# Two-stream attention block on one core: the text gate and text output as one run of 32-column tiles, and the first scales by a transpose

## The chip, the cores and the metric

The kernel runs on one core of a Trainium2 chip. A core has a matrix engine (TensorE), a vector engine (VectorE), a scalar engine (ScalarE), GpSimd and SyncE, and 16 DMA engines which move data between HBM and the on-chip memory SBUF. Matmuls write to a second on-chip memory, PSUM, from which VectorE or ScalarE must take the result ("empty" it). The metric is the device time of one execution in microseconds, the median of several runs. In the profile PE is TensorE's matmuls, PEld its weight loads, DVE VectorE, ACT ScalarE, POOL GpSimd, SP SyncE.

## What is computed

Two streams of tokens, image and text, are normalised, scaled and shifted by vectors made from a conditioning vector `c`, projected to q, k and v, joined for one attention, and projected back with a gate. The reference, cut to what matters:

```python
# B, Ni, Nt, D = 2, 256, 32, 1152; all inputs bf16
mod_i = (silu(c) @ wmod_img).reshape(B, 6, 1, D)      # mod_t likewise from wmod_txt
shi, sci, gai = mod_i[:, 0], mod_i[:, 1], mod_i[:, 2]
sht, sct, gat = mod_t[:, 0], mod_t[:, 1], mod_t[:, 2]
hi = layernorm(x_img) * (1 + sci) + shi
ht = layernorm(x_txt) * (1 + sct) + sht
qkvi, qkvt = hi @ wqkv_img, ht @ wqkv_txt             # split into q, k, v; text and image joined
p = softmax(einsum('bqd,bkd->bqk', q, k) * D ** -0.5)
a = einsum('bqk,bkd->bqd', p, v)
out_i = x_img + gai * (a[:, Nt:] @ wo_img)
out_t = x_txt + gat * (a[:, :Nt] @ wo_txt)
```

## The kernel before

The contraction over D = 1152 runs in KT = 9 steps of 128 rows (`kt` or `dt`). The kernel begins with the layer norm of four image tiles (128 tokens each), transposes them, scales them by `1 + sci` and starts the product for v. Weights stream in on SyncE's DMA queue in the order of use, into five slots that are reused. `pin` keeps an instruction in program order on its engine.

The scales are a product of `silu(c)` with a weight block. `sc_rows` makes them as rows, with four 32-column tiles of the matrix engine side by side (`tile_position`), into `sc_ps`; a VectorE transpose (`sc_cols`) turns them into columns. For the first 128 features the kernel before also makes a column directly, with matmuls two columns wide, and scales the first block from PSUM:

```python
def sc_first(r0, r1):
    if r0 == 0:
        mm(sc0_ps[:], lhsT=warm[:, 0:P], rhs=unit[:, 0:B], start=True, stop=False)
    for kt in range(r0, r1):
        mm(sc0_ps[:], lhsT=w_sc_i[:, kt, 0:P], rhs=sT[:, kt, :], start=False, stop=(kt == KT - 1))

def x_scale(k0, k1, b, step=TPB, first=False):
    for kt in range(k0, k1):
        for t in range(0, TPB, step):
            t0, t1 = b * NI + t * P, b * NI + (t + step) * P
            pin(nc.vector.tensor_scalar(hS_i[:, kt, t0:t1], xT_i[:, kt, t0:t1],
                                        sc0_ps[:, b:b + 1] if first else sc1_i[:, kt, b:b + 1], None,
                                        op0=ALU.mult))
...
sc_rows(0, 4)
sc_first(0, 4)
warm_up(2)                                  # matmuls without use[...]
...                                         # transposes of image tiles 2 and 3 in three parts
sc_first(7, K8)                             # K8 = KT - 1: the last two weight rows
sc_first(K8, KT)
sc_rows(7, KT)
x_scale(0, 1, 0, step=1, first=True)
sc_cols(0, 5)
x_scale(1, 3, 0)
v_open(A0, 0, 3)                            # the first v matmuls, names vps<-t,hS_i
```

The end: the image output is made in four tiles of 128 tokens, each in chunks of up to 384 columns. A chunk is nine matmuls, then a multiplication by the gate out of PSUM (`tmp`) and an addition of x (`o`), both on VectorE. The text gate is one row per batch (`mod_rows`, nine sets of four 32-column matmuls, name `gps`); ScalarE copies it out, GpSimd's DMA queue writes it to DRAM and reads it back spread over the partitions (`gbf`). In the kernel before it runs behind the first chunk of output tile 1, and the text output, with 64-column tiles, between output tiles 2 and 3:

```python
def mod_rows(w_blk):
    gps = ps_mm.tile([P, VC], f32, tag="mm")                    # VC = 288
    for kt in range(KT):
        for g in range(NGG):                                    # NGG = 4
            mm(gps[32 * g:32 * g + 32, :], lhsT=sT32[:, kt, :], rhs=w_blk[:, kt, g * VC:(g + 1) * VC],
               start=(kt == 0), stop=(kt == KT - 1), tile_position=(0, 32 * g))
    return gps

def out_img(i, chunks, parts=None, between=None):
    ...
    for n in chunks:
        if c0 and between:
            between = between()
        ps = ps_mm.tile([P, CH], f32, tag="mm")                 # CH = 384
        for dt in range(KT):
            mm(ps[:, 0:n], lhsT=aT[:, dt, t0:t0 + P], rhs=w_o_i[:, dt, c0:c0 + n],
               start=(dt == 0), stop=(dt == KT - 1))
        tmp = work.tile([P, CH], bf, tag="tmp")
        nc.vector.tensor_mul(tmp[:, 0:n], ps[:, 0:n], gb[:, b, c0:c0 + n])
        nc.vector.tensor_add(o[:, c0:c0 + n], tmp[:, 0:n], x_i[:, i, c0:c0 + n])
        ...                                                     # store of the finished columns

def out_txt():
    of = work.tile([P, 2, VC], bf, tag="of", bufs=1)
    for r in range(2):
        ps = ps_mm.tile([P, VC], f32, tag="mm")
        for dt in range(KT):
            for g in range(2):
                c0 = (2 * r + g) * VC
                mm(ps[64 * g:64 * g + NTT, :], lhsT=aT[:, dt, NI:NI + NTT], rhs=w_o_t[:, dt, c0:c0 + VC],
                   start=(dt == 0), stop=(dt == KT - 1), tile_position=(0, 64 * g))
        tmp = work.tile([P, CH], bf, tag="tmp")
        nc.vector.tensor_mul(tmp[:, 0:VC], ps[:], gbf[:, r, :])
        nc.vector.tensor_add(of[:, r, :], tmp[:, 0:VC], xf[:, r, :])
    ...                                                         # two stores

w_ga_t = load_w(3, wmod_txt, 2 * D)                             # the text gate's weights
w_o_t = load_rows(1, wo_txt, 0, (0, 5))                         # the last weights: dt 0 to 4, then 5 to 8
...
out_img(0, C3)
out_img(1, C3, between=txt_gate)
out_img(2, C3)
out_txt()
out_img(3, (CH, CH, 224, 160), parts=(2 * CH, D - 160, D))
```

Of the kernel before, what the change touches and what calls it, by code (L numbers as in the profile page):

```python
# [14 lines left out]
def kernel(  # L15
# [26 lines left out]
    NTT = B * NT  # L42
    CH = 384
    NCH = D // CH
    VC = 288
# [7 lines left out]
    work = ctx.enter_context(tc.tile_pool(name="work", bufs=2))  # L53
    small = ctx.enter_context(tc.tile_pool(name="small", bufs=4))
    ps_mm = ctx.enter_context(tc.tile_pool(name="ps_mm", bufs=6, space=PSUM))
    ps_tr = ctx.enter_context(tc.tile_pool(name="ps_tr", bufs=2, space=PSUM))

    pin = tc.keep_in_program_order

    def mm(*a, **k):  # L60
        return pin(nc.tensor.matmul(*a, **k))  # L61

    def tr(*a, **k):
        return pin(nc.tensor.transpose(*a, **k))  # L64
# [6 lines left out]
    x_i = act.tile([P, NIT, D], bf)  # L71
# [10 lines left out]
    K8 = KT - 1  # L82
# [17 lines left out]
    w_sc_i = wtile(0)  # L100
# [21 lines left out]
    warm = const.tile([P, 512], bf)  # L122
# [3 lines left out]
    unit = const.tile([P, LW], bf)  # L126
# [41 lines left out]
    sT = const.tile([P, KT, B], bf)  # L168
# [46 lines left out]
    hS_i = act.tile([P, KT, B * NI], bf, tag="Bt")  # L215
    xT_i = act.tile([P, KT, B * NI], bf)
# [8 lines left out]
        pin(nc.vector.transpose(t[:].rearrange("p c l -> p (c l)"), gps[:].rearrange("p c l -> p (c l)")))  # L225
        return t

    sc0_ps = ps_mm.tile([P, B], f32, tag="mm")
    tp60 = ps_mm.tile([P, 3, NI], bf, tag="mm", name="tp")
    tp61 = ps_mm.tile([P, 3, NI], bf, tag="mm", name="tp")  # L230
    sc_ps = ps_mm.tile([P, KT, LW], f32, tag="mm")

    def sc_first(r0, r1):
        if r0 == 0:
            mm(sc0_ps[:], lhsT=warm[:, 0:P], rhs=unit[:, 0:B], start=True, stop=False)
        for kt in range(r0, r1):
            mm(sc0_ps[:], lhsT=w_sc_i[:, kt, 0:P], rhs=sT[:, kt, :], start=False, stop=(kt == KT - 1))

    def sc_rows(r0, r1):
        if r0 == 0:  # L240
            for g in range(NGG):
                mm(sc_ps[LW * g:LW * g + LW].rearrange("p c l -> p (c l)"), lhsT=unit[:], rhs=warm[:, 0:KT * LW],
                   start=True, stop=False, tile_position=(0, LW * g))
        for kt in range(r0, r1):
            for g in range(NGG):
                mm(sc_ps[LW * g:LW * g + LW], lhsT=sT32[:, kt, :], rhs=group(w_sc_i, kt, g),
                   start=False, stop=(kt == KT - 1), tile_position=(0, LW * g))

    def x_tiles(k0, b):
        return (tp61 if b else tp60) if k0 == 6 else ps_tr.tile([P, 3, NI], bf, tag="tr", name="tp")  # L250

    def x_transposes(tp, k0, b, ts=range(TPB)):
        for kt in range(k0, k0 + 3):
            for t in ts:
                i = b * TPB + t
                tr(tp[:, kt - k0, t * P:(t + 1) * P], xn_i[:, i, kt * P:(kt + 1) * P], ident[:])

    def x_out(tp, k0, b):
        dst = xT_i[:, k0:k0 + 3, b * NI:(b + 1) * NI]
        pin(nc.vector.tensor_copy(dst, tp[:]) if k0 == 3 else nc.scalar.copy(dst, tp[:]))  # L260

    sc1_i = const.tile([P, KT, LW], f32, name="scc", tag="scc")

    def sc_cols(c0, c1):
        pin(nc.vector.transpose(sc1_i[:, c0:c1, :].rearrange("p c l -> p (c l)"),
                                sc_ps[:, c0:c1, :].rearrange("p c l -> p (c l)")))

    def x_scale(k0, k1, b, step=TPB, first=False):
        for kt in range(k0, k1):
            for t in range(0, TPB, step):  # L270
                t0, t1 = b * NI + t * P, b * NI + (t + step) * P
                pin(nc.vector.tensor_scalar(hS_i[:, kt, t0:t1], xT_i[:, kt, t0:t1],  # L272
                                            sc0_ps[:, b:b + 1] if first else sc1_i[:, kt, b:b + 1], None,
                                            op0=ALU.mult))

    VW = 512
# [26 lines left out]
    ln_var(s0)  # L303
    ln_norm_dve(1, m1)
    ln_norm_act(0, s0)
    tps = [(x_tiles(k0, 0), k0, 0) for k0 in (3, 0, 6)]
    for tp in tps:
        x_transposes(*tp)
    s2 = ln_sums(x_i[:, 2, :], xn_i[:, 2, :])
    m3 = ln_stats(x_i[:, 3, :], P)  # L310
    ln_var(s2)
    x_out(*tps[0])
    r3, r2 = ln_rstd(m3[:, 1:2], P), ln_rstd(s2[:, 2:3], P, sign=-1.0)
    ln_norm(x_i[:, 3, :], m3[:, 0:1], r3, P, xn_i[:, 3, :])
    ln_norm(x_i[:, 2, :], s2[:, 0:1], r2, P, xn_i[:, 2, :])
    x_out(*tps[1])
    x_out(*tps[2])
    sc_rows(0, 4)
    sc_first(0, 4)
    warm_up(2)  # L320
    t3, t0, t6 = [(x_tiles(k0, 1), k0, 1) for k0 in (3, 0, 6)]
    x_transposes(*t3, ts=(1,))
    x_transposes(*t6, ts=(1,))
    sc_rows(4, 7)
    sc_first(4, 7)
    x_transposes(*t3, ts=(0,))
    x_transposes(*t6, ts=(0,))
    x_transposes(*t0)
    x_out(*t3)
    x_out(*t6)  # L330
    x_out(*t0)
    sc_first(7, K8)
    sc_first(K8, KT)
    sc_rows(7, KT)
    x_scale(0, 1, 0, step=1, first=True)
    sc_cols(0, 5)
    x_scale(1, 3, 0)
    v_open(A0, 0, 3)
    x_scale(0, 3, 1)
    sc_cols(5, KT)  # L340
    for k0 in (3, 6):
# [361 lines left out]
    for dts in ((0, 5, 1), (6, 2, 7), (3, 8, 4)):  # L703
        attn_pair(*[[(b, dt) for dt in dts] for b in range(B)])

    def out_img(i, chunks, parts=None, between=None):
        b = i // TPB
        t0 = b * NTOK + qpos[b][i % TPB]
        o = work.tile([P, D], bf, tag="o")
        c0 = s0 = 0  # L710
        for n in chunks:
            if c0 and between:
                between = between()
# [5 lines left out]
            nc.vector.tensor_mul(tmp[:, 0:n], ps[:, 0:n], gb[:, b, c0:c0 + n])  # L719
            nc.vector.tensor_add(o[:, c0:c0 + n], tmp[:, 0:n], x_i[:, i, c0:c0 + n])  # L720
            c0 += n
            if parts is None and c0 == D or parts and c0 in parts:
                (nc.scalar if parts and c0 == D else nc.sync).dma_start(oi_v[b, i % TPB, :, s0:c0], o[:, s0:c0])
                s0 = c0

    def out_txt():
        of = work.tile([P, 2, VC], bf, tag="of", bufs=1)
        for r in range(2):
            ps = ps_mm.tile([P, VC], f32, tag="mm")
            for dt in range(KT):  # L730
                for g in range(2):
                    c0 = (2 * r + g) * VC
                    mm(ps[64 * g:64 * g + NTT, :], lhsT=aT[:, dt, NI:NI + NTT], rhs=w_o_t[:, dt, c0:c0 + VC],
                       start=(dt == 0), stop=(dt == KT - 1), tile_position=(0, 64 * g))
            tmp = work.tile([P, CH], bf, tag="tmp")
            nc.vector.tensor_mul(tmp[:, 0:VC], ps[:], gbf[:, r, :])
            nc.vector.tensor_add(of[:, r, :], tmp[:, 0:VC], xf[:, r, :])
        for g in range(2):
            eng = nc.sync if g == 0 else nc.scalar
            eng.dma_start(ot_flat.rearrange("t (r g j) -> g t r j", r=2, g=2)[g], of[64 * g:64 * g + NTT, :, :])  # L740

    C3 = (CH, CH, CH)
    out_img(0, C3)
    out_img(1, C3, between=txt_gate)
    out_img(2, C3)
    out_txt()
    out_img(3, (CH, CH, 224, 160), parts=(2 * CH, D - 160, D))


# [28 lines left out]
```

## Time and profile before

| | us |
|---|---|
| median of 3 runs | 117.93 (117.65 to 118.27) |
| span of the profiled execution | 115.9 |
| first v matmul starts | 14.17 |
| text gate rows on TensorE, first start | 97.21 |
| text output on TensorE, weight loads from | 105.84 |
| last store issued | 113.43 |

The profile's span runs from the first to the last instruction; the device time is some 2 us longer. Times inside the kernel count from the start of the span. The profile's page gives busy time by engine and a row of slices; the chain that ended last goes back from the last instruction to what released each step; a timeline line gives start, duration, engine, source line, operation, the tiles written and read, and in brackets the idle time before it with what ended it. Matmuls overlap: one of 384 columns is shown as 326 ns long, but the next starts 0.1625 us after it (36 of them, two output tiles' first chunks, take 5.85 us in the chain).

### The profile page before, as it was taken

What the parts mean: (1) busy time and instruction counts of PE and PEld (TensorE: products, weight loads), DVE (VectorE), ACT (ScalarE), POOL (GpSimd) and SP (SyncE); (2) the same over time, 40 slices, a digit from 0 to 9 for tenths busy, and PEclk for the clock granted to TensorE, in tenths of its full rate; (3) what the DMA queues carried; (4) which work ended last, traced back from release to release, by engine and by line L of the source; (5) the groups of instructions that cost most, each with busy time, mean ns of one, the idle gap of its engine ahead of it and who ended that gap; (6) DMA issues with size and microseconds to landing.
All of it is one profiled execution on the core that took longest, in us unless ns stands there. A gap on an engine that the chain in (4) does not pass through costs nothing.

```text
span 115.9 us, 2586 instructions
## 1 busy us (share of the span) xinstructions
PE 109.9 (95%) x1081; PEld 63.3 (55%) x1081; DVE 72.0 (62%) x152; ACT 44.0 (38%) x92; POOL 12.4 (11%) x34
## 2 busy tenths in 40 slices
PE   4978899999999999999999999999999999999990
PEld 2325644445574444445454458887866565557670
DVE  3469692063869999999996040018758509466571
ACT  4699810041752279825241223244657400100000
POOL 7300000000000000000000000003432600415000
PEclk9999999999999999999999999999999999999999
DMA  4999999999999999999999999999999999941223
GB/s 110 362 379 396 406 404 412 412 413 410 412 400 411 292 404 407 410 410 414 410 350 400 409 405 414 411 410 406 415 402 407 406 416 370 390 167 51 102 51 102
DMA packets 18917, 41.02 MB, mean 354 GB/s; under 512 B 1323, under 2 KB 1851, under 8 KB 18907
## 3 DMA queue, kind: packets, MB, share of 16 engines
q1 hardware_dynamic: 18032, 39.85, 89.7%
q0 software_dynamic: 480, 0.89, 2.1%
q10 hardware_dynamic: 395, 0.12, 0.4%
q8 instruction: 8, 0.13, 0.4%
q14 instruction: 2, 0.02, 0.0%
HBM read 39.52 MB, written 1.34 MB: 353 GB/s over the span
## 4 chain that ended last, share of the span: by engine, by line
PE 84%; ACT 5%; DMA 3%; DVE 3%; issue 1%; DVEq 0%
PE ps L61 52%; PE vps L61 15%; PE gps L61 5%; PE aps L61 5%; PE sps L61 4%; DMA x_i<-in_x_img_dram 3%; ACT xn_i L197 2%; ACT xn_i L198 2%; DVE tmp L719 1%; DVE xT_i L260 1%; DVE o L720 1%; PE tp L64 1%; ACT pT L639 1%; PE sc_ps L61 1%; DVE xn_i L212 0%
## 5 line engine op out<-in xcount | busy, mean ns | idle before, releaser
L61 PE MATMUL ps<-xT_i,t 128*128 128x512 bf16 x162 | 35.7, 379 | 0.0
L61 PEld LDWEIGHTS <-t 128*128 128x128 bf16 x333 | 20.9, 98 | 19.1 <-issue 0.7
L453 DVE SCALAR_TENSOR_TENSOR acc_sh<-t,sTf,acc_sh 128x1152 f32<-128x1152 bf16 x16 | 21.4, 1411 | 0.0
L61 PE MATMUL ps<-t,aT 128*128 128x384 bf16 (+3 forms) x153 | 20.3, 308 | 0.0
L61 PE MATMUL vps<-t,hS_i 128*128 128x512 bf16 (+1 forms) x108 | 17.9, 326 | 0.1
L61 PEld LDWEIGHTS <-aT 128*128 128x128 bf16 (+1 forms) x153 | 13.0, 101 | 7.1 <-issue 0.8
L61 PEld LDWEIGHTS <-hS_i 128*128 128x128 bf16 x108 | 9.0, 98 | 8.9 <-DVE hS_i L272 0.6
L719 DVE TENSOR_TENSOR tmp<-ps,gb 128x384 bf16<-128x384 f32 (+2 forms) x13 | 6.8, 525 | 7.9 <-PE ps L61 4.5
L383 ACT CAST qkT<-ps 128x512 bf16<-128x512 f32 (+2 forms) x11 | 6.1, 552 | 14.8 <-PE ps L61 13.5
L605 POOL TENSOR_SCALAR pb<-e,rs 128x32 bf16<-128x32 f32 (+1 forms) x5 | 2.2, 446 | 75.8 <-DVE rs L602 75.8
L381 ACT ACTIVATE qkT<-ps 128x512 bf16<-128x512 f32 (+2 forms) x11 | 5.9, 559 | 8.1 <-PE ps L61 6.5
L61 PE MATMUL wps<-warm 128*128 128x512 bf16 x24 | 7.2, 453 | 1.5 <-DVE unit L127 1.5
L180 DVE CAST v_i<-vps 128x512 bf16<-128x512 f32 x5 | 3.5, 692 | 7.9 <-PE vps L61 7.9
L590 DVE TENSOR_REDUCE nmx<-sps 128x1 f32<-128x288 f32 x4 | 1.8, 458 | 9.4 <-PE sps L61 9.4
L182 ACT CAST v_i<-vps 128x512 bf16<-128x512 f32 x4 | 2.3, 580 | 10.0 <-PE vps L61 10.0
L652 DVE TENSOR_SCALAR aT<-aps,svc 128x288 bf16<-128x288 f32 x9 | 4.3, 517 | 2.2 <-PE aps L61 2.2
L61 PEld LDWEIGHTS <-sT 128*32 128x32 bf16 x180 | 4.4, 96 | 1.8 <-issue 1.2
L61 PE MATMUL sps<-qkT 128*128 128x288 bf16 (+1 forms) x54 | 5.3, 287 | 0.0
L61 PE MATMUL gps<-t,sT 128*32 128x288 bf16 x144 | 5.2, 287 | 0.0
L61 PEld LDWEIGHTS <-warm 128*128 128x128 bf16 x25 | 2.6, 112 | 4.8 <-issue 1.9
L61 PE MATMUL aps<-pT,v_i 128*128 128x288 bf16 x36 | 5.1, 287 | 0.1
L61 PE MATMUL ps<-hT_t,t 128*128 128x64 bf16 x162 | 5.0, 193 | 0.0
(114 smaller groups left out, 105.5 us busy)
## 6 DMA issues: line engine op xcount, KB each, us to landing
t<-in_wqkv_txt_dram SPq DMA_DIRECT2D x3, 2592.0 KB, 19.6
t<-in_wmod_img_dram SPq DMA_DIRECT2D x2, 2592.0 KB, 13.9
t<-in_wmod_txt_dram SPq DMA_DIRECT2D x2, 2592.0 KB, 19.1
t<-in_wqkv_img_dram SPq DMA_DIRECT2D x3, 864.0 KB, 13.7
t<-in_wqkv_img_dram SPq DMA_DIRECT2D x1, 2592.0 KB
t<-in_wo_img_dram SPq DMA_DIRECT2D x3, 864.0 KB, 10.4
t<-in_wqkv_img_dram SPq DMA_DIRECT2D x3, 576.0 KB, 9.9
t<-in_wmod_txt_dram SPq DMA_DIRECT2D x2, 864.0 KB, 13.8
```

What stands on the lines that cost most here:

```text
L61: return pin(nc.tensor.matmul(*a, **k))
L180: nc.vector.tensor_copy(out_ap, in_ap)
L182: nc.scalar.copy(out_ap, in_ap)
L197: pin(nc.scalar.activation(junk, x_ap, ACT.Copy, scale=1.0 / D, accum_out=sm[:, 0:1]))
L198: pin(nc.scalar.activation(junk, x_ap, ACT.Square, scale=float(D) ** -0.5, accum_out=sm[:, 1:2]))
L381: nc.scalar.mul(out_ap, in_ap, SCALE)
L383: nc.scalar.copy(out_ap, in_ap)
L453: pin(nc.vector.scalar_tensor_tensor(acc, w_sh_t[:, kt, :], col, acc, op0=ALU.mult, op1=ALU.add))
L590: pin(nc.vector.reduce_max(nmx[0:qn, :], sps[0:qn, :], axis=AX.X, negate=True))
L605: pin(nc.gpsimd.tensor_scalar(pb[0:qn, NI + 2 * NT:NI + 3 * NT], e[0:qn, NI:NTOK], rs[0:qn, :], 0.0, op0=ALU.mult, op1=ALU.add))
L652: nc.vector.tensor_scalar(dst, tiles[(b, dt)][:], bias, None, op0=ALU.add)
L719: nc.vector.tensor_mul(tmp[:, 0:n], ps[:, 0:n], gb[:, b, c0:c0 + n])
```

## The change

Two things are done. At the start, the direct column for the first block's scales is taken out: the first block is scaled from the transposed rows, for which the first 32 columns are transposed by themselves, and the transposes of the image tiles go back to three whole groups, the last behind the scale rows. At the end, the text gate rows move behind output tile 1 and the text output follows them at once, itself in 32-column tiles (one per batch and half), so that all of it is one run in one tiling of the matrix engine. The text result stays in PSUM, in the pool that the transposes used, and VectorE empties it behind output tile 2, when the gate has been spread. VectorE's output instructions are pinned to program order.

```diff
-    def sc_first(r0, r1):
-        ...
+    def x_transposes(k0, b):
+        tr_pool = b == 1 or k0 < 6
+        tp = (ps_tr if tr_pool else ps_mm).tile([P, 3, NI], bf, tag="tr" if tr_pool else "mm", name="tp")
         ...
     ...
-    x_out(*tps[0])                       # ahead of the norms of tiles 3 and 2
     ...
     sc_rows(0, 4)
-    sc_first(0, 4)
-    warm_up(2)
-    ...                                  # transposes in parts, sc_first(4, 7)
-    sc_first(7, K8)
-    sc_first(K8, KT)
-    sc_rows(7, KT)
-    x_scale(0, 1, 0, step=1, first=True)
-    sc_cols(0, 5)
+    warm_up(3)
+    sc_rows(4, 7)
+    out01 = x_transposes(0, 1)
+    out31 = x_transposes(3, 1)
+    sc_rows(7, K8)
+    sc_rows(K8, KT)
+    out61 = x_transposes(6, 1)
+    out01()
+    sc_cols(0, 1)
+    x_scale(0, 1, 0, step=1)
+    sc_cols(1, 5)
     x_scale(1, 3, 0)
     v_open(A0, 0, 3)
+    out31()
+    out61()
     ...
-            nc.vector.tensor_mul(tmp[:, 0:n], ps[:, 0:n], gb[:, b, c0:c0 + n])
+            pin(nc.vector.tensor_mul(tmp[:, 0:n], ps[:, 0:n], gb[:, b, c0:c0 + n]))
     ...                                  # and so for the other three
     def out_txt():
+        tiles = []
         for r in range(2):
-            ps = ps_mm.tile([P, VC], f32, tag="mm")
+            ps = ps_tr.tile([P, VC], f32, tag="tr", name="txo")
             for dt in range(KT):
                 for g in range(2):
-                    c0 = (2 * r + g) * VC
-                    mm(ps[64 * g:64 * g + NTT, :], lhsT=aT[:, dt, NI:NI + NTT], ...
-                       start=(dt == 0), stop=(dt == KT - 1), tile_position=(0, 64 * g))
+                    for b in range(B):
+                        c0, r0, t0 = (2 * r + g) * VC, 64 * g + NT * b, NI + NT * b
+                        mm(ps[r0:r0 + NT, :], lhsT=aT[:, dt, t0:t0 + NT], ...
+                           start=(dt == 0), stop=(dt == KT - 1), tile_position=(0, r0))
+            tiles.append(ps)
+        return tiles
+
+    def out_txt_store(tiles):            # the multiplication, the addition and the stores
     ...
     out_img(0, C3)
-    out_img(1, C3, between=txt_gate)
+    out_img(1, C3)
+    txt_gate()
+    txt = out_txt()
     out_img(2, C3)
-    out_txt()
+    out_txt_store(txt)
     out_img(3, (CH, CH, 224, 160), parts=(2 * CH, D - 160, D))
```

More of the change, by code (lines that the diff above doesn't have):

```diff
@@ L226, in mod_cols_of @@
         return t
-    sc0_ps = ps_mm.tile([P, B], f32, tag="mm")
-    tp60 = ps_mm.tile([P, 3, NI], bf, tag="mm", name="tp")
-    tp61 = ps_mm.tile([P, 3, NI], bf, tag="mm", name="tp")
     sc_ps = ps_mm.tile([P, KT, LW], f32, tag="mm")
-    def sc_first(r0, r1):
[L234 to L237, printed above, removed]
     def sc_rows(r0, r1):
@@ L247, in sc_rows, with copy_out @@
                    start=False, stop=(kt == KT - 1), tile_position=(0, LW * g))
-    def x_tiles(k0, b):
-        return (tp61 if b else tp60) if k0 == 6 else ps_tr.tile([P, 3, NI], bf, tag="tr", name="tp")
-    def x_transposes(tp, k0, b, ts=range(TPB)):
+    def x_transposes(k0, b):
+        tr_pool = b == 1 or k0 < 6
+        tp = (ps_tr if tr_pool else ps_mm).tile([P, 3, NI], bf, tag="tr" if tr_pool else "mm", name="tp")
         for kt in range(k0, k0 + 3):
-            for t in ts:
+            for t in range(TPB):
                 i = b * TPB + t
                 tr(tp[:, kt - k0, t * P:(t + 1) * P], xn_i[:, i, kt * P:(kt + 1) * P], ident[:])
-    def x_out(tp, k0, b):
         dst = xT_i[:, k0:k0 + 3, b * NI:(b + 1) * NI]
-        pin(nc.vector.tensor_copy(dst, tp[:]) if k0 == 3 else nc.scalar.copy(dst, tp[:]))
+        def copy_out():
+            pin(nc.vector.tensor_copy(dst, tp[:]) if k0 == 3 else nc.scalar.copy(dst, tp[:]))
+        return copy_out
     sc1_i = const.tile([P, KT, LW], f32, name="scc", tag="scc")
@@ L266, in sc_cols, with x_scale @@
                                 sc_ps[:, c0:c1, :].rearrange("p c l -> p (c l)")))
-    def x_scale(k0, k1, b, step=TPB, first=False):
+    def x_scale(k0, k1, b, step=TPB):
         for kt in range(k0, k1):
@@ L271, in x_scale @@
                 t0, t1 = b * NI + t * P, b * NI + (t + step) * P
-                pin(nc.vector.tensor_scalar(hS_i[:, kt, t0:t1], xT_i[:, kt, t0:t1],
-                                            sc0_ps[:, b:b + 1] if first else sc1_i[:, kt, b:b + 1], None,
+                pin(nc.vector.tensor_scalar(hS_i[:, kt, t0:t1], xT_i[:, kt, t0:t1], sc1_i[:, kt, b:b + 1], None,
                                             op0=ALU.mult))
@@ L305 @@
     ln_norm_act(0, s0)
-    tps = [(x_tiles(k0, 0), k0, 0) for k0 in (3, 0, 6)]
-    for tp in tps:
-        x_transposes(*tp)
     s2 = ln_sums(x_i[:, 2, :], xn_i[:, 2, :])
@@ L315 @@
     ln_norm(x_i[:, 2, :], s2[:, 0:1], r2, P, xn_i[:, 2, :])
-    x_out(*tps[1])
-    x_out(*tps[2])
+    for out in [x_transposes(k0, 0) for k0 in (0, 3, 6)]:
+        out()
     sc_rows(0, 4)
-    sc_first(0, 4)
-    warm_up(2)
-    t3, t0, t6 = [(x_tiles(k0, 1), k0, 1) for k0 in (3, 0, 6)]
-    x_transposes(*t3, ts=(1,))
-    x_transposes(*t6, ts=(1,))
-    sc_rows(4, 7)
[L325 to L331, printed above, removed]
-    sc_first(7, K8)
-    sc_first(K8, KT)
-    sc_rows(7, KT)
-    x_scale(0, 1, 0, step=1, first=True)
-    sc_cols(0, 5)
+    warm_up(3)
+    sc_rows(4, 7)
+    out01 = x_transposes(0, 1)
[7 more added lines that the diff above has]
+    sc_cols(1, 5)
     x_scale(1, 3, 0)
     v_open(A0, 0, 3)
+    out31()
+    out61()
     x_scale(0, 3, 1)
@@ L704, with out_img @@
         attn_pair(*[[(b, dt) for dt in dts] for b in range(B)])
-    def out_img(i, chunks, parts=None, between=None):
+    def out_img(i, chunks, parts=None):
         b = i // TPB
@@ L711, in out_img @@
         for n in chunks:
-            if c0 and between:
-                between = between()
             ps = ps_mm.tile([P, CH], f32, tag="mm")
@@ L718, in out_img @@
             tmp = work.tile([P, CH], bf, tag="tmp")
-            nc.vector.tensor_mul(tmp[:, 0:n], ps[:, 0:n], gb[:, b, c0:c0 + n])
-            nc.vector.tensor_add(o[:, c0:c0 + n], tmp[:, 0:n], x_i[:, i, c0:c0 + n])
+            pin(nc.vector.tensor_mul(tmp[:, 0:n], ps[:, 0:n], gb[:, b, c0:c0 + n]))
+            pin(nc.vector.tensor_add(o[:, c0:c0 + n], tmp[:, 0:n], x_i[:, i, c0:c0 + n]))
             c0 += n
@@ L726, in out_txt @@
     def out_txt():
-        of = work.tile([P, 2, VC], bf, tag="of", bufs=1)
+        tiles = []
         for r in range(2):
-            ps = ps_mm.tile([P, VC], f32, tag="mm")
+            ps = ps_tr.tile([P, VC], f32, tag="tr", name="txo")
             for dt in range(KT):
                 for g in range(2):
-                    c0 = (2 * r + g) * VC
-                    mm(ps[64 * g:64 * g + NTT, :], lhsT=aT[:, dt, NI:NI + NTT], rhs=w_o_t[:, dt, c0:c0 + VC],
-                       start=(dt == 0), stop=(dt == KT - 1), tile_position=(0, 64 * g))
+                    for b in range(B):
+                        c0, r0, t0 = (2 * r + g) * VC, 64 * g + NT * b, NI + NT * b
+                        mm(ps[r0:r0 + NT, :], lhsT=aT[:, dt, t0:t0 + NT], rhs=w_o_t[:, dt, c0:c0 + VC],
+                           start=(dt == 0), stop=(dt == KT - 1), tile_position=(0, r0))
+            tiles.append(ps)
+        return tiles
+    def out_txt_store(tiles):
+        of = work.tile([P, 2, VC], bf, tag="of", bufs=1)
+        for r, ps in enumerate(tiles):
             tmp = work.tile([P, CH], bf, tag="tmp")
-            nc.vector.tensor_mul(tmp[:, 0:VC], ps[:], gbf[:, r, :])
-            nc.vector.tensor_add(of[:, r, :], tmp[:, 0:VC], xf[:, r, :])
+            pin(nc.vector.tensor_mul(tmp[:, 0:VC], ps[:], gbf[:, r, :]))
+            pin(nc.vector.tensor_add(of[:, r, :], tmp[:, 0:VC], xf[:, r, :]))
         for g in range(2):
```

## Prediction

> **What bounds the kernel now.** I read the page first: busy times, then the row of DMA rates, then the shares of the chain that ended last.
>
> ```profile
> PE 109.9 (95%) x1081; PEld 63.3 (55%) x1081; DVE 72.0 (62%) x152; ACT 44.0 (38%) x92; POOL 12.4 (11%) x34
> ...
> GB/s 110 362 379 396 406 404 412 412 413 410 412 400 411 292 404 407 410 410 414 410 350 400 409 405 414 411 410 406 415 402 407 406 416 370 390 167 51 102 51 102
> ...
> PE 84%; ACT 5%; DMA 3%; DVE 3%; issue 1%; DVEq 0%
> ```
>
> See two things here. TensorE is busy 95% and carries 84% of the chain. And DMA runs at about 410 GB/s in nearly every slice up to slice 34 of 40 (a slice is 2.9 us), that is to about 102 us: weights arrive just in time until then. So a TensorE instruction that is moved earlier in the last quarter may find its weights missing. Next, the chain in order of time (start, duration, what):
>
> ```profile
> 13.23 0.56 DVE xT_i L260
> 13.79 0.01 DVEq L272
> 13.80 0.05 issue
> 13.85 0.27 DVE hS_i L272
> 14.12 0.05 issue
> 14.17 13.77 PE vps L61 x63
> ...
> 81.02 1.10 PE gps L61 x36
> 82.12 2.21 PE ps L61 x72
> ...
> 97.28 1.22 PE gps L61 x36
> 98.50 12.79 PE ps L61 x99
> 111.29 0.02 issue
> 111.31 0.57 DVE tmp L719
> ```
>
> From 14.17 to 111.29 the chain is on TensorE but for one 1.2 us piece at 84.8. Before 14.17 it is a chain of small steps, after 111.31 it is VectorE. The change touches both ends. Third, the answer for the text output's weights: two transfers, when they were issued, and how long the second took to land.
>
> ```profile
> L97 SPq DMA_DIRECT2D t<-in_wo_txt_dram x2: 368/816/1264, 84.4 to 84.8; - x2
> ...
> DMA to landing us min/median/max: 17.6/17.6/17.6
> ```
>
> The second piece (rows dt = 5 to 8) was issued at 84.8 and lands at 84.8 + 17.6 = 102.4 us. In the kernel before, the text output starts at 105.85, so nobody waits for it. Last, the timeline of VectorE at the end:
>
> ```profile
> 107.55 0.46 DVE L736 TENSOR_TENSOR tmp<-ps,gbf 128x288 bf16<-128x288 f32 x1 [0.65 <-DMA gbf<-mod_scratch]
> 108.04 0.31 DVE L737 TENSOR_TENSOR of<-tmp,xf 128x288 bf16<-128x288 bf16 x1
> ...
> 109.85 0.56 DVE L719 TENSOR_TENSOR tmp<-ps,gb 128x384 bf16<-128x384 f32 x1 [0.76 <-PE ps L61]
> 110.44 0.36 DVE L720 TENSOR_TENSOR o<-tmp,x_i 128x384 bf16<-128x384 bf16 x1
> ```
>
> VectorE idles before most of its work here, 0.76 us before the first piece of output tile 3: it has room while TensorE does the text output, and none after 111.31.
>
> **What the Trainium skill says.** "TensorEngine Tiling (Array Packing)", Key Properties: changing the tiling mode drains TensorE, moving between tiles of one mode doesn't. The trace agrees: a set of four 32-column matmuls takes 1.10 / 9 = 0.122 us in the run at 81.02, where the mode was already 32 columns; the gate rows between output chunks (97.28) take 1.22, one switch more. The same page, PSUM Bottleneck: tiling speeds up TensorE but not what empties PSUM. That is the point of my last step. "DMA: Bandwidth & Descriptors", Queues, rings and completion order: each DMA engine consumes a ring's descriptors in order. Here the weights all go through one queue, and the text output's are the last, so their landing is set by the bytes ahead of them, not by who needs them.
>
> **The change, part by part.** *A, the start.* Removed: ten 2-column matmuls (the column of scales); they ran while TensorE was waiting for rows and for normalised tokens anyway, so I count nothing for them. In their place the first block's scales come through a 32-column transpose on VectorE. Before, the last weight row of the scale block (issued 3.7, the single-row pieces take 9.7 us, so landed 13.4) is used at once by a 2-column matmul; VectorE scales from 13.85, TensorE starts the v product at 14.17, 0.32 later. After: TensorE waits for the same row until about 13.40, then a set of four, ending 0.29 later (duration of one) at 13.69; VectorE starts 0.04 later, 13.73; the transpose of 32 columns takes about 0.22 (343 ns for 160 columns and 311 for 128 give 1 ns a column and 0.18 fixed), and its reader follows 0.04 later, at 13.98; TensorE starts at 14.30. The six transposes left on TensorE end by about 14.2 (each 0.056 apart, behind a ScalarE copy of 0.8 that starts near 12.95), so they hide. Step A: **+0.15 us**, between 0.05 and 0.3.
>
> *B, the switches.* Gate before: the last 128-column matmul starts at 96.96, the next would have started 0.1625 later, at 97.12; the gate's first starts at 97.21, and the output goes on at 98.43. That is 1.31 for 9 x 0.122 = 1.10, so 0.21 for two switches. Text before: 105.75 (the last start, 105.59, and 0.1625) to 108.17, when output tile 3 begins, 2.42 for 18 pairs of 64-column matmuls at 0.122 = 2.20, again 0.22. After: 27 sets of four at 0.122 = 3.31 and two switches, 0.21: 3.52 against 3.74. The text's matmuls double in count (36 to 72) but the run of 72 at 82.12 shows 2.21 us, the same as 36 wider ones. Step B: **-0.22 us** on TensorE.
>
> *C, the weights of the text output.* The gate moves behind the last two chunks of output tile 1: 18 matmuls at 0.1625 = 2.93, so it starts at 97.21 + 2.93 + 0.15 (A) = 100.29; the text starts 1.10 later at 101.39, dt = 5 is reached five sets later at 102.00. The first piece of the weights is there by 99.5 (102.4 less 1152 KB at 410 GB/s), the second lands at 102.4, seen by TensorE at about 102.45. Step C: **+0.45 us** of waiting. The load is on a queue that is full since the start, so I take its landing as fixed; then A is swallowed, because a later TensorE only waits less. The rest is 13 sets (1.59) and a switch (0.11): output tile 2 starts at 104.15, tile 3 another 27 matmuls on (4.39 and 0.01), at 108.55, against 108.17 before: **+0.38**. A + B + C says the same.
>
> *D, VectorE at the end.* The text's result is now emptied behind output tile 2, so between the last piece of tile 2 and the first of tile 3. A piece of 384 columns holds VectorE 0.87 (start to next start: 97.16 to 98.02, 95.43 to 96.30), the two text pairs 1.50 together (107.55 to where the next could start, 109.05), the 224- and 160-column pieces 0.62 and 0.63. Tile 2's last piece starts 4.59 after the tile does (before: 101.36 and 105.95), so at 108.74; the text at 109.61; tile 3's first piece at 111.11, while TensorE has it ready at 108.55 + 1.68 = 110.23. Second piece 111.98 (ready 111.69), third 112.85, fourth 113.47, last store issued 114.10. Before: 113.43. Of these 0.67, 0.38 is TensorE's and **0.29** the backlog that VectorE cannot work off: it is 0.88 late at the first piece, gains 0.59 on the second (0.87 of work against TensorE's 1.46), and the last two follow back to back, as they do before.
>
> The gate's broadcast must be there at 109.61. Gate rows end at 101.7; the ScalarE cast and the two writes go out 0.7 and 1.3 later, land after 2 us if the queue is empty by then, and the four broadcasts need 2.2 to issue and 2.0 to land: about 108.3. Hidden, with 1.3 us to spare, but not by much.
>
> The sum is +0.67 on the last store; what follows it is unchanged. 117.93 + 0.67 = 118.6. I shade it to **118.5**, because C and D rest on differences of 0.3 us between much longer times.
>
> **Rivals.** *R1, the switches win:* the weights of the text land earlier than 102.0, or the tile is not waited for; then TensorE is 0.07 ahead (A and B), D alone acts, and the time is 117.93 - 0.07 + 0.29 = 118.15. For it: the landing is a single number from one execution; against it: the full DMA row up to 102. *R2, VectorE is no bound:* D falls away if the pairs overlap more than I read; with C alone the time is 118.3, with neither C nor D 117.85, the only way to a gain. Against it: in the chain VectorE already ends the kernel from 111.31 on. *R3, the broadcast becomes the wait:* if it lands at 110.6, everything from there is a microsecond later, 119.5. Its 4.3 us for the same writes before (99.2 to 103.5) speak for it, but then the queue still had weights in it. *R4, the start costs more:* a further 0.3 in A is covered by C, so it shows nowhere.
>
> **Range and chances.** 118.15 to 118.6 without surprises; the times before spread over 0.6 us, and R3 and R2 add a tail on each side. I take 117.9 to 119.1 for 8 in 10. Two per cent is 2.4 us, which no step comes near: faster by over 2% 0.01, within 2% 0.97, slower by over 2% 0.02.
>
> **What would show it.** A: the v product starts at about 14.3 instead of 14.17. B: gate rows and text as one run of 27 sets, with a switch only at its ends. C: within that run, a gap of about 0.4 us after five text sets, ended by the text weights; if there is none, C is wrong. D: tile 3's first piece starts on VectorE without idle time before it, about 0.9 after TensorE finished it, and the chain's last stretch on VectorE is longer than before, from the text pieces on. R3 would show as VectorE waiting for the gate's broadcast before the first text piece. The prediction fails altogether if the weight transfers shift as a whole, for then C has no fixed point.

## The result, and the profile after

| | before | after |
|---|---|---|
| median of 6 runs, us | 118.03 (117.65 to 118.27) | 118.57 (118.37 to 118.71) |
| span of the profiled execution | 115.9 | 116.5 |

The changed kernel takes 1.0046 times as long as the one before, with a 95% interval of 1.0025 to 1.0066: half a microsecond more, within the range that was stated and almost at its centre. The page of the changed kernel, the same three lines as before the change:

```profile
PE 111.0 (95%) x1108; PEld 63.8 (55%) x1108; DVE 71.7 (62%) x153; ACT 44.0 (38%) x92; POOL 12.4 (11%) x34
...
GB/s 93 371 375 401 404 408 408 414 410 412 411 400 411 293 389 407 407 412 411 411 354 391 410 414 414 404 412 404 408 407 409 404 417 378 359 149 25 32 145 101
...
PE 67%; DMA 23%; DVE 4%; SPq 1%; issue 1%; DVEq 0%
```

Busy times hardly differ. What differs is the third line: TensorE's share of the chain that ended last fell from 84% to 67%, and DMA's rose from 3% to 23%. The chain now rests on two transfers, because TensorE waits for both. The shares say nothing of how long it waits: the chain counts a transfer from its issue, the second with 17.26 us, for a wait of 0.24 (below). In order of time (start, duration, what):

```profile
2.12 9.78 DMA t<-in_wmod_img_dram
11.90 0.04 issue
11.95 0.55 PE sc_ps L61 x12
12.50 0.78 PE tp L64 x12
13.27 0.47 PE sc_ps L61 x8
13.74 0.02 issue
13.77 0.23 DVE scc L257
...
14.09 0.27 DVE hS_i L264
14.35 0.05 issue
14.40 13.77 PE vps L61 x63
...
67.51 8.74 PE ps L61 x180
76.26 5.13 PE sps L61 x54
...
85.17 17.26 DMA t<-in_wo_txt_dram
102.42 0.04 issue
102.47 1.78 PE txo L61 x52
104.24 4.51 PE ps L61 x27
108.75 0.02 issue
108.77 0.57 DVE tmp L699
```

At the start the transpose (`scc`) stands between the scale rows and the first scaling, and the v product begins at 14.40. At the end the text output (`txo`) goes on at 102.47, when the second piece of its weights has landed (85.17 + 17.26 = 102.43). From 108.77 on the chain is on VectorE, 2.5 us earlier than before. The timeline of VectorE from there:

```profile
109.64 0.45 DVE L723 TENSOR_TENSOR tmp<-txo,gbf 128x288 bf16<-128x288 f32 x1
110.13 0.31 DVE L724 TENSOR_TENSOR of<-tmp,xf 128x288 bf16<-128x288 bf16 x1
110.35 0.45 DVE L723 TENSOR_TENSOR tmp<-txo,gbf 128x288 bf16<-128x288 f32 x1
110.84 0.31 DVE L724 TENSOR_TENSOR of<-tmp,xf 128x288 bf16<-128x288 bf16 x1
111.06 0.55 DVE L699 TENSOR_TENSOR tmp<-ps,gb 128x384 bf16<-128x384 f32 x1
```

No bracket with idle time stands behind any of these lines, neither behind the first text piece (so the gate's broadcast was there) nor behind the first piece of output tile 3 at 111.06, which was preceded by 0.76 us of idle time before.

### The profile page after: what moved, and what is told of

Its sections match the earlier page's. It is cut to its first block, busy times and chain, and to the rows that moved or that the text cites. A ratio compares the mean times of both kernels' runs of the same rounds, so it can differ in the third digit from the quotient of the medians.

```text
span 116.5 us, 2641 instructions
## 1 busy us (share of the span) xinstructions
PE 111.0 (95%) x1108; PEld 63.8 (55%) x1108; DVE 71.7 (62%) x153; ACT 44.0 (38%) x92; POOL 12.4 (11%) x34
## 4 chain that ended last, share of the span: by engine, by line
PE 67%; DMA 23%; DVE 4%; SPq 1%; issue 1%; DVEq 0%
PE ps L61 40%; PE vps L61 15%; DMA t<-in_wo_txt_dram 15%; DMA t<-in_wmod_img_dram 8%; PE sps L61 4%; PE gps L61 4%; DVE tmp L699 2%; PE txo L61 2%; DVE o L700 1%; PE sc_ps L61 1%; DVE tmp L723 1%; SPq L104 1%; PE tp L64 1%; SPq L108 0%; SPq L97 0%
## 5 line engine op out<-in xcount | busy, mean ns | idle before, releaser
L61 PE MATMUL ps<-t,aT 128*128 128x384 bf16 (+2 forms) x117 | 17.9, 314 | 0.0
L61 PE MATMUL wps<-warm 128*128 128x512 bf16 x25 | 8.4, 499 | 1.5 <-DVE unit L127 1.5
```

## Experiments

Three terms were to be told apart: the start (A), the wait for the text's weights (C) and VectorE's backlog (D); the switches (B) can be read off a timeline. Ratios are against the kernel before, run beside them on the same chip. Chips and executions differ by some tenths of a microsecond, much of it in when the first transfers land, so I also compare distances inside one profile. From the first v matmul to the last store it is 99.26 us in the kernel before (113.43 - 14.17) and 99.62 in the changed one (114.02 - 14.40). Here are the last stores in the two timelines, before and changed, and below them a part of the chain before:

```profile
113.43 0.39 ACTq L723 DMA_DIRECT2D out_dram<-o  x1
114.02 0.39 ACTq L703 DMA_DIRECT2D out_dram<-o  x1
```

```profile
67.28 8.61 PE ps L61 x180
75.89 5.13 PE sps L61 x54
```

The end alone is better read from the attention scores (`sps`) on, for the stretch before them also differs between executions. From there to the last store it is 37.54 us before and 37.76 after, 0.22 more. The 180 matmuls for q and k ahead of `sps` account for another 0.13 (8.74 against 8.61). That is a part of the new start's cost: in all six profiles of the new start TensorE stands at one and the same matmul there, 0.03 to 0.21 us longer than between its neighbours (0.12 in the changed kernel), and in none of the eight of the old start. The profile shows no wait for it, and its cause stays open.

**The new start alone.** The changed kernel up to the attention products, with the end of the kernel before:

```diff
     # from the kernel before
     ...                                  # out_txt and the unpinned VectorE operations likewise
-    txt_gate()
-    txt = out_txt()
+    out_img(1, C3, between=txt_gate)
     out_img(2, C3)
-    out_txt_store(txt)
+    out_txt()
```

> The start of the changed kernel with the end of the kernel before. Theory M (the prediction's terms): the start costs 0.23 us (v product at 14.40 instead of 14.17), and since the old end waits for no weights it passes through in full: 118.03 + 0.23 = 118.26, the text output starts 0.2 later. Rival N (the weights' queue is the anchor of the whole kernel, so a later start is made up at some wait): no change, 118.0.

Ratio 1.0037 (1.0018 to 1.0056). The start costs something by itself, and the old end passes it on: rival N falls. The expected 1.002 lies in the interval, at its lower end, for it left out the pause in the middle, which is 0.2 here; the end from `sps` on is the old one, 37.54. The chain shows the piece of 180 broken in two:

```profile
68.25 7.36 PE ps L61 x137
75.60 0.03 issue
75.64 1.43 PE ps L61 x43
```

In its profile the last scale row landed 0.75 us later than in the kernel before, so the start is better read from that row on. TensorE in this run:

```profile
13.93 0.52 PE L61 MATMUL sc_ps<-t,sT 128*32 128x288 bf16 x8
14.55 0.49 PE L64 MATMUL tp<-ident,xn_i 128*128 128x128 bf16 x6
15.13 0.61 PE L61 MATMUL vps<-t,hS_i 128*128 128x512 bf16 x2
```

The row landed at 14.10, the v product starts 1.03 later. In the changed kernel it is 13.37 and 14.40, again 1.03; in the kernel before 13.35 and 14.17, 0.82. But there TensorE did not wait for the row: its two-column matmuls stood behind the transposes and ran at 13.54, and the scaling at 13.85 came after VectorE's copy of the transposed tokens, which ended at 13.79. In three later profiles of the old start TensorE did wait for the row, and the v product starts 0.77 to 0.78 after the landing. So from a row that both wait for, the new start costs 0.25 us; against the kernel before, with its own bound, 0.21 from the row and 0.23 on the profile's clock.

**The new end alone.** The old start with the changed end.

```diff
     # to the kernel before
     ...                                  # out_txt and the pinned VectorE operations of the changed kernel
     out_img(0, C3)
-    out_img(1, C3, between=txt_gate)
+    out_img(1, C3)
+    txt_gate()
+    txt = out_txt()
     out_img(2, C3)
-    out_txt()
+    out_txt_store(txt)
```

> The start of the kernel before with the end of the changed kernel. Theory M: the text's fifth set is reached 0.25 to 0.4 earlier but waits until the weights land at 102.4, so output tile 2 starts at 104.15 as in the changed kernel and the time is the same, 118.5 to 118.6; the wait inside the run is then about 0.5. Rival (the costs of start and end add): 118.57 - 0.23 = 118.34.

Ratio 1.0043 (1.0015 to 1.0071), the same as the whole change, though the start's cost is not in it. The timeline of TensorE shows the weights as the reason:

```profile
100.99 0.79 PE L61 MATMUL txo<-t,aT 128*32 128x288 bf16 x20
102.02 1.78 PE L61 MATMUL txo<-t,aT 128*32 128x288 bf16 x52 [0.25 <-DMA t<-in_wo_txt_dram]
```

Five sets of four start, and the sixth, due at 100.99 + 5 x 0.122 = 101.60, starts at 102.02. (The bracket gives 0.25, since a matmul is shown until its last column has passed, 0.29 us.) So TensorE stood 0.42 here, against 0.24 in the changed kernel, where the run starts at 101.62 and the sixth set was due at 102.23. The two intervals are too wide to exclude that the costs add; the two waits are what shows that most of the later start was paid out of the wait. From `sps` to the last store it is 37.93 here: the 0.39 more than before are the sum of -0.22 (switches), 0.42 (wait) and 0.21 (VectorE, below), within 0.02.

**The wait taken away.** In the new end, the text output does the first five steps of both halves before the last four of either; the second piece of weights is needed five sets later.

```diff
-        for r in range(2):
-            ps = ps_tr.tile([P, VC], f32, tag="tr", name="txo")
-            for dt in range(KT):
+        tiles = [ps_tr.tile([P, VC], f32, tag="tr", name="txo") for r in range(2)]
+        for dts in ((0, 5), (5, KT)):
+            for r in range(2):
+                for dt in range(*dts):
```

With the start of the kernel before:

> As the run with the new end alone, but the text output does dt 0 to 4 for both halves first and then dt 5 to 8, so that the second piece of weights is needed 0.6 later. Theory M: no wait for weights, output tile 2 starts at about 103.55 instead of 104.15; the backlog on VectorE stays. 118.57 - 0.6 = 117.95, unless the gate's broadcast (landed at 109.08 in the changed kernel, while VectorE would now want it at 109.0) takes over as the wait: then up to 118.2. Rival (the wait for weights is hidden behind VectorE's backlog): unchanged, 118.5.

Ratio 1.0021 (1.0001 to 1.0041). And with the start of the changed kernel:

> The changed kernel with the text output's dt 0 to 4 first for both halves. Theory M: the wait of 0.24 inside the run is gone, output tile 2 starts that much earlier, VectorE's backlog stays: 0.25 less than the changed kernel, ratio 1.0025. Rival (the wait is made up behind it, by the broadcast of the gate or by VectorE): unchanged, 1.0045.

Ratio 1.0032 (1.0014 to 1.0050). TensorE in this last run, gate and text without a gap:

```profile
101.07 1.29 PE L61 MATMUL gps<-t,sT 128*32 128x288 bf16 x36
102.18 2.38 PE L61 MATMUL txo<-t,aT 128*32 128x288 bf16 x72
104.49 0.82 PE L61 MATMUL ps<-t,aT 128*128 128x384 bf16 x4
```

The wait is gone from both profiles and both ratios are lower than with it, by 0.0022 and 0.0014; the intervals overlap, so the size of the gain is not settled by the times alone. I had expected more of the first one (0.6 us, 0.9993): the wait in the run before it was 0.42, not 0.6, and 0.0022 of the time is 0.26. The profiles are sharper than the times: from `sps` to the last store it is 37.51 and 37.52 in these two runs, so that without the wait the new end is as long as the old one (37.54), what the switches save being lost again on VectorE. For the changed start's run, with 0.23 at the start and 0.22 in the middle, the profile's sum gives a ratio of 1.0036, as measured; for the old start's it gives 0.9997, just below the interval, and where the other 0.3 us are is not known. The lines also give B: from the first gate matmul to the next output tile 3.42, and 0.09 for the switch ahead of it, 3.51, to be set against 3.74 for gate and text before.

**Gate and text apart again.** As the first of these two, but with the gate back behind the first chunk of output tile 1 (`out_img(1, C3, between=txt_gate)`).

> Start of the kernel before, new end with dt 0 to 4 first, but the text gate back behind the first chunk of output tile 1, so that gate and text are two runs of 32-column tiles with four switches. Theory M: gate and text together take 3.73 on TensorE as in the kernel before, instead of the 3.51 of one run. Rival (32-column sets themselves are faster or slower than the 64-column pairs): another sum than 3.73.

A single execution, without an interval. TensorE:

```profile
97.25 1.29 PE L61 MATMUL gps<-t,sT 128*32 128x288 bf16 x36
98.46 3.10 PE L61 MATMUL ps<-t,aT 128*128 128x384 bf16 x18
101.49 2.47 PE L61 MATMUL txo<-t,aT 128*32 128x288 bf16 x72
103.89 0.50 PE L61 MATMUL ps<-t,aT 128*128 128x384 bf16 x2
```

Gate 1.21, text 2.40, and 0.09 ahead of each: 3.79. Of this some 0.09 is a wait for weights (the eleventh set was due at 102.72, its weights landed at 102.75). Without it 3.70, as expected and as in the kernel before: two runs cost two switches more, and the sum leaves no room for a difference between sets of four 32-column matmuls and pairs of 64.

**VectorE without the text.** First the text's four operations were left out altogether and `x_txt` stored as the text output, so that gate and product of the text stream are missing.

> The changed kernel without its four text operations on VectorE; x_txt is stored as the text output, so gate and product of the text stream are left out of it (TensorE still does them). Theory M: VectorE's backlog before output tile 3 is gone, the last store is issued 0.87 after TensorE's last matmul as in the kernel before, instead of 1.11, and the time is 0.25 to 0.3 below the changed kernel: ratio 1.002. Rival (VectorE is no bound there): unchanged, 1.0045.

The run took 133.02 us and says nothing of D. ScalarE's queue held one of the stores, and the scheduler had put it ahead of the attention's copies:

```profile
97.40 0.63 ACTq L723 DMA_DIRECT2D out_dram<-xf  x1
98.07 1.18 ACT L621 COPY pT<-pT_ps 128x576 bf16<-128x576 bf16 x2 [14.51 <-DMA xf<-in_x_txt_dram]
```

A store that waits in an engine's instruction stream holds up all that follows: ScalarE stood 14.51 us for `xf`. The second attempt gives the store something to wait for at the right place:

```diff
         for r, ps in enumerate(tiles):
-            tmp = work.tile([P, CH], bf, tag="tmp")
-            pin(nc.vector.tensor_mul(tmp[:, 0:VC], ps[:], gbf[:, r, :]))
-            pin(nc.vector.tensor_add(of[:, r, :], tmp[:, 0:VC], xf[:, r, :]))
+            pin(nc.scalar.copy(of[:, r, :], ps[:]))
```

> The changed kernel with the text result copied out of PSUM by ScalarE and stored as it is: gate and residual of the text stream are left out, so VectorE has no text operations and the text stores go out early. Theory M: the last store is issued 0.9 behind the last matmul's start as in the kernel before, instead of 1.11, and 0.29 earlier against the first v matmul than in the changed kernel; ratio 1.0046 - 0.0025 = 1.002. Rival (VectorE's backlog was no bound): unchanged, 1.0045.

Ratio 1.0026 (1.0013 to 1.0039). VectorE at output tile 3:

```profile
109.86 0.56 DVE L699 TENSOR_TENSOR tmp<-ps,gb 128x384 bf16<-128x384 f32 x1 [0.51 <-PE ps L61]
110.46 0.36 DVE L700 TENSOR_TENSOR o<-tmp,x_i 128x384 bf16<-128x384 bf16 x1
111.33 0.56 DVE L699 TENSOR_TENSOR tmp<-ps,gb 128x384 bf16<-128x384 f32 x1 [0.51 <-PE ps L61]
```

VectorE waits for TensorE again before each piece, and the last store is issued 0.90 after the last matmul's start, as in the kernel before; in the changed kernel it was 1.11. D is there, with 0.21 instead of the 0.29 foretold. Against the first v matmul the store gained only 0.17 (99.45 for 99.62), since TensorE came to the text's weights earlier against their landing and waited 0.34 instead of 0.24. The ratio is lower than the changed kernel's 1.0046, but the intervals overlap and the chips differ; D rests on the profile.

**The text's work on another engine.** Here nothing is left out: ScalarE empties PSUM, GpSimd multiplies and adds, on the old start and the new end without the wait for weights.

```diff
-            pin(nc.vector.tensor_mul(tmp[:, 0:VC], ps[:], gbf[:, r, :]))
-            pin(nc.vector.tensor_add(of[:, r, :], tmp[:, 0:VC], xf[:, r, :]))
+            pin(nc.scalar.copy(cp[:, r, :], ps[:]))       # cp: a tile of its own
+        for r in range(2):
+            nc.gpsimd.tensor_mul(cp[:, r, :], cp[:, r, :], gbf[:, r, :])
+            nc.gpsimd.tensor_add(of[:, r, :], cp[:, r, :], xf[:, r, :])
```

> As the one before, and the text result is emptied from PSUM by ScalarE and multiplied and added on GpSimd, so that VectorE has only the image chunks at the end. Theory M: the backlog of 0.29 goes, output tile 3's first piece waits for TensorE again: 117.95 - 0.3 = 117.65, below the kernel before. Rival (GpSimd takes VectorE's share of SBUF and slows it, or its own four operations last longer than until 112.5 and become the end): 118.0 or more.

Ratio 1.0101 (1.0055 to 1.0148): the rival's side in the time, but neither of its reasons shows: the last store is issued 99.04 after the first v matmul, 0.22 earlier than in the kernel before, about as expected, and GpSimd is done at 110.7. Yet the span goes on for 3.35 us from there instead of 2.45, for the last store takes 2.4 us to land instead of 1.6. The store of output tile 2 had come to stand behind a text store on SyncE's queue and went out with the last ones. So the text stores were moved to ScalarE's queue (`nc.scalar.dma_start` for both), with the old start and with the changed one:

> As the GpSimd run before it (start of the kernel before, new end, dt 0 to 4 first, text result by ScalarE and GpSimd), but both text stores are issued on ScalarE's queue, so that the store of output tile 2 doesn't stand behind them on SyncE's. Theory M with late stores as the cause of the lost microsecond: the stores of tile 2 go out at about 108.7 again, the last store is issued 0.2 earlier than in the kernel before, and the time is 0.2 below it (ratio 0.998). Rival (GpSimd's work on the text slows the end by itself): still 0.5 to 1.0 above.

> The changed kernel with all its work, the text result emptied by ScalarE, multiplied and added on GpSimd and stored from ScalarE's queue. Theory M: as without VectorE's text operations, ratio 1.002. Rival (GpSimd and VectorE share SBUF and VectorE's additions slow down noticeably, or GpSimd ends too late): 1.0045 or more.

Ratios 1.0046 (1.0021 to 1.0070) and 1.0093 (1.0065 to 1.0121). The first is lower than in the run with the late store, though the intervals overlap, and both are still above the kernel before. The store of tile 2 goes out at 109.39 again, so its lateness was not what held up the last one. Of the old start's run, the store of the last columns in the answer on DMA (count, size, microseconds from issue to landing), and below it VectorE:

```profile
out_dram<-o ACTq DMA_DIRECT2D x1, 40.0 KB, 2.4
```

```profile
108.54 0.82 DVE L718 TENSOR_TENSOR o<-tmp,x_i 128x384 bf16<-128x384 bf16 x1
```

In the kernel before the same store took 1.6 us to land. GpSimd needs 3.0 us for its four operations, so the text stores go out at 111.5 and 112.1 and not at 109.1, and the last image store, 1.5 and 0.9 us behind them, takes 0.8 longer. It takes 2.3 to 2.4 us in all three runs with GpSimd and 1.5 to 1.6 in every other profile, so the late text stores fit as the cause; whether their nearness or the shared queue does it was not tried.

While GpSimd works, VectorE's addition takes 0.82 us instead of 0.36. "SBUF — State Buffer" of the Trainium skill, SBUF: two separate sides, says that a VectorE operation with two inputs in SBUF and a GpSimd operation that reads SBUF exclude each other. The traces agree: the six additions that met a GpSimd operation in the three runs took 0.38 to 0.84 us, and each ended 0.21 to 0.22 after the end of that operation. It cost nothing in the old start's runs, where the last store was issued as early as foretold, for VectorE had slack there. The rivals were right about the result: relieving VectorE by GpSimd delays the text stores, and the last store then takes longer.

**A version from these findings.** VectorE keeps the text, but the gate comes sooner, and its pairs are spread: one between the second and third piece of output tile 2, one behind the third. Old start, no wait for weights:

```diff
-            nc.gpsimd.dma_start(gsc[si, b, :]...)
+            eng = nc.scalar if si == 1 and b == 0 else nc.gpsimd
+            pin(eng.dma_start(gsc[si, b, :]...))
-                nc.gpsimd.dma_start(gbf[r0:r0 + NT, :, :], ...)
+                eng = nc.gpsimd if b else nc.scalar
+                pin(eng.dma_start(gbf[r0:r0 + NT, :, :], ...))
     ...                                          # txt_ops(r): one pair of out_txt_store's operations
-    out_img(2, C3)
-    out_txt_store(txt)
+    out_img(2, C3, hook=lambda: txt_ops(0))      # ahead of the third piece's multiplication
+    txt_ops(1)
+    out_txt_store()                              # stores on GpSimd's and ScalarE's queues
```

> Start of the kernel before, new end with dt 0 to 4 first, and VectorE's text work spread: the gate's second write and two of its four broadcasts go through ScalarE's queue, so that the gate should be there near 107 instead of 108.7; the first text pair runs between the second and third piece of output tile 2, the second pair behind the third; text stores on GpSimd's and ScalarE's queues. Theory M: no wait for weights, no backlog left at tile 3's second piece, the text stores go out before 110; the last store is issued 99.05 after the first v matmul, as against 99.26 in the kernel before; ratio 0.998. If the gate isn't there by 107.4, the first pair holds up tile 2's third piece and the ratio is 1.000 or more.

Ratio 1.0029 (1.0013 to 1.0045), a miss. Inside the profile all went as planned: the first text pair starts at 107.64 without waiting, and the last store is issued 99.02 after the first v matmul, 0.24 earlier than in the kernel before. But behind it SyncE waits for the stores' semaphores one after the other, about 0.06 us each, in a fixed order. In the kernel before the last store's is the last of them, and the program ends 0.82 us after its landing was seen (115.00 to 115.82). Moving transfers between queues had given the last store another semaphore, early in that order: six waits followed it, 1.18 us (114.83 to 116.01). The 0.36 more, less the 0.24 gained, leave 0.12 us, a ratio of 1.001, just below the interval: the closing waits are a part of the loss, and the rest is not explained. The last run gives the last store its old semaphore back, by moving two stores:

```diff
-                (nc.scalar if parts and c0 == D else nc.sync).dma_start(oi_v...)
+                (nc.scalar if parts and c0 == D else nc.gpsimd if i == 0 else nc.sync).dma_start(oi_v...)
-            pin((nc.gpsimd if g == 0 else nc.scalar).dma_start(ot_flat...))
+            pin(nc.gpsimd.dma_start(ot_flat...))
```

> As the run with VectorE's text work spread, but with the store of output tile 0 and both text stores on GpSimd's queue, so that the last store's landing is again the last of SyncE's closing waits, as in the kernel before (there SyncE's closing waits go on for 1.2 us after that landing was seen, here for 0.8). Theory M: last store 99.0 after the first v matmul against 99.26, closing waits as before: 0.2 below the kernel before, ratio 0.998. Rival (something else in the new end costs time outside the chain): 1.000 to 1.003 as in the run with the text work spread.

Ratio 0.9968 (0.9947 to 0.9988): the one version that beats the kernel before, 117.83 against 118.29 on the same chip (the changed kernel was not run there). How it does so is not settled. The closing waits are back at 0.82 us (115.42 to 116.24), as expected. But the profiled execution is otherwise not the expected one: the text's weights landed at 103.09 there, 0.7 us later than in the kernel before; the last scale row was late by 0.37 already, and the rest is perhaps due to the first output store, which now travels on another queue beside them. TensorE waited again in the middle of the text, and the last store was issued 99.40 after the first v matmul, not 99.0. This run and the one before it were also taken on different chips, so their difference cannot all be put down to the closing waits.

## Why the prediction was right, point by point

**The time.** 118.5 was said, 118.57 measured. The last store was to move by 0.67 and moved by 0.59 (113.43 to 114.02), the span by 0.6. The measured terms are 0.23 (A), 0.13 (the pause in the middle), -0.22 (B), 0.24 (C) and 0.21 (D), together 0.59. The mechanism is thus borne out term by term, but the closeness of the two times is in part luck: the 0.1 by which 118.6 was shaded had no term behind it, and the measured difference is 0.54 us with an interval of 0.3 to 0.8.

**A, the start.** Right in kind, a little small: 0.15 foretold, 0.23 in the profile (14.40). Most of the error is the gap between the transpose and its reader: the transpose starts at 13.77 (13.73 foretold) and takes 0.22 as estimated, but the scaling starts at 14.09, 0.11 after its end instead of 0.04. The prediction also misread what the old start waits for: not the last row, used "at once", but VectorE's copy until 13.79. The number hardly suffered, for the cost was counted from the measured 14.17. The pause in the middle was not foreseen at all. (The piece off TensorE at 84.8 in the chain before is 0.7 us, not 1.2; nothing rests on it.)

**B, the switches.** Right: 3.51 for one run of 27 sets, to 3.52 foretold, and 3.70 for two runs.

**C, the weights.** Right in place and end, wrong in length: the sixth set was foretold for 102.45 and started at 102.47, but the wait was 0.24 and not 0.45, because TensorE arrived 0.23 later. Of that, 0.08 is A, and 0.13 was lost in the middle of the kernel, where the 180 q and k matmuls took 8.74 us instead of 8.61 at a granted clock of 1.00 in both profiles. The prediction's remark that a later TensorE only waits less held twice, here and with the old start (0.42). It made the sum insensitive to the error in A and to the pause: output tile 2 starts at 104.17, foretold 104.15.

**D, VectorE.** Right in kind, 0.21 instead of 0.29. The text pairs hold VectorE 1.42 (109.64 to 111.06), not 1.50: the working took them from a stretch in which the second pair had to wait for its matmuls and nothing was queued behind it. The first piece of tile 3 starts at 111.06, foretold 111.11, and the last store goes out at 114.02, foretold 114.10.

**The rivals.** R1 is excluded by the wait, R2 by the missing idle time and by the 0.21 us that the last store gained on the last matmul when the text was taken off VectorE. R3 did not come true: the last broadcast landed at 109.08, 0.56 before VectorE wanted it, later than the estimated 108.3; the two writes landed 2.6 and 2.1 us after their issue, not the 4.3 of the kernel before. R4 held: what the start costs more, in the middle too, disappears in C; where no weights were waited for, with the old end, it showed.

## What to carry to other kernels

Before work on the matrix engine is moved earlier, look up when its operands land: here joining two runs saved 0.22 us of switches and met a weight transfer that had landed some 4 us before its use until then. Ask the same of what comes behind: the engine that empties the results had room where the work stood and none where it was put. And when an engine's load is moved, follow the stores it feeds to the very end of the program, for in the runs with GpSimd text stores that went out 2 us later came with a last store that took 0.8 us longer, more than the 0.22 that was saved. A change at the start can also cost time far from it: here 8.61 us of unchanged matmuls became up to 8.83.

## What the runs showed that I had not expected

The end of the program is not free of order: with the same 1.54 to 1.56 us from issue to landing of the last store, the closing waits of SyncE took 0.82 or 1.18 us, depending on which semaphore that store used. And a 40 KB store, issued 1.5 and 0.9 us behind two stores of 72 KB, took 2.4 us to land instead of 1.6.
